# Attention and a top-2 expert layer on one core: the decay moved into the casts of q and k, a router in smaller steps, and late weights cast one part at a time

## The chip, the core and the metric

The kernel runs on one core of a Trainium2 chip. PE is TensorE, which multiplies matrices; DVE is VectorE, ACT is ScalarE, POOL is GpSimd, and SP only issues transfers. Each engine works through its own queue in the order in which the program gives it work, and waits on semaphores for the others. The metric is device time in microseconds (us) for one execution, lower being better; the kernel before was run three times: 549.3, 549.66 and 552.47, median 549.66.

## What is computed

The first half is attention with a decay in place of a softmax, for 8 batches, 8 heads, 576 positions and 64 values a head. The second half sends each of the 4608 tokens to two of eight experts, each two matrix products with a ReLU between.

```python
scores = scale * np.matmul(q, k.transpose(0, 1, 3, 2))
gamma = 1.0 - 2.0 ** (-5.0 - np.arange(H, dtype=np.float32))
Dmat = np.where(rel >= 0, gamma[:, None, None] ** rel[None, :, :], 0.0)
x = np.matmul(scores * Dmat[None], v)          # tokens x 512
noisy = x @ w_gate + np.log1p(np.exp(x @ w_noise)) * noise
# of the two best experts of a token, weights p by softmax:
out[token] += p * (np.maximum(x[token] @ w1[e], 0.0) @ w2[e])
```

The decay gamma^(i-j) for a query at i and a key at j splits into a factor for the query and one for the key.

## The kernel before

The attention is cut into 16 units `u`: a unit is one batch and four heads (two pairs `hp`), of the first 512 positions. The last 64 positions of a batch, its tail, are done for two batches at once (`bp`, four of them). The main loop runs n = 0 to 16; in pass n unit n has its scores and its states computed and unit n - 1 its output. Raw q, k and v are loaded four units ahead on SP's queue, into four buffers each, and `cast(u + 2)` turns them to bf16 two units ahead (`kn`, `vn` in three buffers, `qb` in two):

- k by two selects with a condition that is always true, on POOL (L194), v by a multiply with its share of the decay, gamma^-j, on POOL (L199), q by an ACT copy with the factor 0.125 (L203);
- `tr` (L249, L251) transposes q and k on PE and copies the result from PSUM on ACT (`QT`, `KT`);
- `scores` (L264, L270) multiplies, and DVE applies the causal mask;
- `states` (L286, L292) sums key by value over blocks of positions into `T`, which ACT copies to the block-diagonal `Tb`;
- `out` (L312, L320, L326) brings scores and states together, and DVE multiplies by the query's share of the decay (`gt`) on the way from PSUM to `xT`. `scores_tail` (L337) and `out_tail` (L351) do this for tails, one pair of heads at a time; `cast_tail` (L215 to L221) and `tr_tail` prepare them.

Between these, `step()` stands seven times in a pass. Each call runs the router of a finished batch pair up to its next `yield`. `route` computes logits by PE (L489), the two largest by DVE, the running counts `cum` on POOL (L543), ranks within an expert by a product with a triangular matrix (L576, L578), a payload `pl` for each token (L563 to L568, L628 to L633), a sort key `key` (L612 to L615), one-hot matrices `olo` and `oh` (L642 to L652), and with these, on PE (L658), the list of tokens of each expert. `row` (L483, L484) transposes the tokens back, to go to DRAM as `xd`. A router is put in line at the end of pass 4, 8, 12 and 16.

When three routers are done, the generator `early` is started, which runs five expert tiles of 256 tokens; `more()` gives it one step, at each `step()` of pass 16 and of the loop behind it that ends the last router. Then the token list is finished, indirect DMAs on POOL gather the rows of the first tiles (L823), and `experts` runs the 35 late tiles: `g1` of tile i + 1 is interleaved with `g2` of tile i on PE (L942, L961); the hidden values are evacuated by ACT and DVE in turn (L947, L949) from three `p` buffers; results of first visits go to `yd` by SP, second visits fetch them by an indirect DMA (`prv`, L969), add (L997) and are scattered to the output (L1003).

Weights of experts 2 to 7 come during tiles 0 to 23: `wload(i + 1)` at the end of tile i loads two parts of 512 KB on SP's queue into `wst` (four buffers), and `wcast` at the end of the next tile turns both to bf16 on ACT (L892). Constants are made ahead of the decay tables (`decay_tables`, L110 to L127), among them `gt` of 576 columns for each of eight heads; POOL sets `Tb` to zero (L161) and loads the gate weights with a cast to bf16 (L1105, L1106).

Of the kernel before, what the change touches and what calls it, by code (L numbers as in the profile page):

```python
# [43 lines left out]
HD = 64  # L44
NC9 = 9
# [58 lines left out]
def decay_tables(nc, cp, tmp):  # L104

    vg = cp.tile([P, 2, 2, 4, 2], F32, name="vg")
    vgt = cp.tile([P, 8], F32, name="vgt")
    gt = cp.tile([P, 4, 576], F32, name="gt")
    tv = tmp.tile([P, 576], F32, name="tv", bufs=1)
    nc.gpsimd.iota(tv[:, :512].rearrange("p (c r q) -> p c r q", c=4, r=4), pattern=[[P, 4], [1, 4], [4, 32]],  # L110
                   base=0, channel_multiplier=0, allow_small_or_imprecise_dtypes=True)
    nc.gpsimd.iota(tv[:, 512:], pattern=[[1, HD]], base=512, channel_multiplier=0,
                   allow_small_or_imprecise_dtypes=True)
    sv = tmp.tile([P, 2, 2], F32, name="sv")
    nc.gpsimd.iota(sv, pattern=[[256, 2], [1, 2]], base=0, channel_multiplier=2,
                   allow_small_or_imprecise_dtypes=True)
    st = tmp.tile([P, 1], F32, name="st")
    for b in range(2):
        nc.gpsimd.iota(st[b * HD:(b + 1) * HD], pattern=[[0, 1]], base=512, channel_multiplier=1,
                       allow_small_or_imprecise_dtypes=True)  # L120
    for h in range(8):
        lng = math.log(1.0 - 2.0 ** (-5.0 - h))
        hp, hi = h // 2, h % 2
        s = slice(hi * HD, (hi + 1) * HD)
        nc.scalar.activation(vg[:, h // 4, :, h % 4, :], sv, Act.Exp, scale=-lng)
        nc.scalar.activation(vgt[:, h:h + 1], st, Act.Exp, scale=-lng)
        nc.scalar.activation(gt[s, hp, :], tv[s], Act.Exp, scale=lng)  # L127
    return vg, vgt, gt


class Attention:
# [26 lines left out]
    def tables(self):  # L158
        self.vg, self.vgt, self.gt = decay_tables(self.nc, self.cp, self.bf)
        for t in self.Tb:  # L160
            self.nc.gpsimd.memset(t, 0.0)  # L161
# [24 lines left out]
    def cast(self, u):  # L186

        nc = self.nc
        d = self.u[u]
        hq = self.unit(u)[1]  # L190
        kn = self.bf.tile([P, 2, 2, 4, HD], BF16, name="kn", bufs=3)
        rk = d.pop("rawk").rearrange("p c h (r d) -> p (c h) r d", r=2)
        for r in range(2):
            nc.gpsimd.affine_select(kn[:, r].rearrange("p c h d -> p (c h) d"), rk[:, :, r, :],  # L194
                                    pattern=[[0, 8], [0, HD]], base=1, channel_multiplier=0,
                                    compare_op=Alu.is_gt, fill=0.0)
        vn = self.bf.tile([P, 2, 2, 4, HD], BF16, name="vn", bufs=3)
        rv = d.pop("rawv").rearrange("p c h (r d) -> p (c h) r d", r=2)
        nc.gpsimd.tensor_tensor(vn.rearrange("p r c h d -> p (c h) r d"), rv,  # L199
                                self.vg[:, hq].rearrange("p c h r -> p (c h) r").unsqueeze(3).to_broadcast(  # L200
                                    [P, 8, 2, HD]), Alu.mult)
        qb = self.bf.tile([P, 4, 4, HD], BF16, name="qb")
        nc.scalar.activation(qb.rearrange("p r h d -> p h r d"),  # L203
                             d.pop("rawq").rearrange("p c h w -> p (c h w)").rearrange("p (h r d) -> p h r d", h=4, r=4),
                             Act.Copy, scale=0.125)
        d.update(kn=kn, vn=vn, qb=qb)

    def cast_tail(self, bp):
        nc = self.nc
        d = {}  # L210
        for n in "qk":
            t = self.bf.tile([P, DM], BF16, name=n + "t", bufs=1)
            a = self.tails.pop((n, bp)).rearrange("p h d -> p (h d)")
            if n == "q":
                nc.scalar.activation(t, a, Act.Copy, scale=0.125)  # L215
            else:
# [1007 lines left out]
```

## Time and profile before

| what | value |
|---|---|
| median of three runs | 549.66 us |
| profiled execution | 599.09 us, span 597.5 us |
| granted TensorE clock, mean | 0.847 |
| busy: PE, DVE, ACT, POOL | 454.6, 277.8, 268.2, 274.3 us |
| attention and routers, to the end of unit 15 | 0 to 196.1 us |
| last router, early tiles, first gathers | 196.1 to 270 us |
| late expert tiles | 270 to 580 us |
| moved by DMA | 104.18 MB, 174 GB/s |

The profiled execution is slower than the median, so stages are compared inside it. A busy time is the sum of an engine's instructions in a stretch of time; an engine that is busy for nearly all of a stretch sets its length, while one with much idle time only does so if others wait for it at the wrong moment. In a list of groups the mean duration of one instruction stands behind the busy time, and behind the bar the idle time of the engine ahead of these instructions, with what ended it. The line of an ACT or DVE instruction in a timeline tells which part of which unit is being done.

### The profile page before, as it was taken

Reading aid. Unit: us, or ns where it says so; the run is one execution under the profiler, and the core shown is the slowest. Engines: PE = TensorE matmul, PEld = TensorE weight load, DVE = VectorE, ACT = ScalarE, POOL = GpSimd, SP = SyncE. Lnnn points to the kernel's source line nnn. Section 1 sums busy time; section 2 is a strip of 40 time slices with the busy share of each in tenths; the row PEclk is TensorE's granted clock in tenths of the full one; section 3 lists DMA queues with packets and bytes.
Section 4 is the critical chain, followed back from the end, with each engine's and each line's share of the span. In section 5 each row is a group of like instructions: output and inputs, shape, how many; then the busy total and the mean of one; then the engine's idle time right before and its main releaser. Section 6 shows DMA issues by size and latency. Waiting matters only on the chain.

```text
span 597.5 us, 11717 instructions
## 1 busy us (share of the span) xinstructions
PE 454.6 (76%) x4587; PEld 315.4 (53%) x4627; DVE 277.8 (46%) x770; ACT 268.2 (45%) x381; POOL 274.3 (46%) x350
## 2 busy tenths in 40 slices
PE   0687738828756678968998799799798798989960
PEld 0565626616644455645665366366464464656630
DVE  0266796796778278313333143243233243344430
ACT  5657716723660365534563464464444451312200
POOL 8753543335232605570246216336347256666660
PEclk9989758655875697988999699799799698999995
DMA  9995999709446313730677567577575643544450
GB/s 239 285 238 119 249 297 265 223 0 259 73 72 130 92 41 125 261 118 17 219 257 251 164 218 235 173 253 232 183 269 183 218 135 114 166 129 130 146 176 20
DMA packets 96170, 104.18 MB, mean 174 GB/s; under 512 B 25447, under 2 KB 73065, under 8 KB 96112
## 3 DMA queue, kind: packets, MB, share of 16 engines
q1 hardware_dynamic: 79824, 69.51, 39.4%
q0 software_dynamic: 15232, 32.84, 20.0%
q10 hardware_dynamic: 1056, 1.05, 0.5%
q8 instruction: 37, 0.61, 0.4%
q14 instruction: 21, 0.17, 0.1%
HBM read 84.66 MB, written 28.72 MB: 190 GB/s over the span
## 4 chain that ended last, share of the span: by engine, by line
PE 25%; issue 17%; POOL 5%; DMA 3%; DVE 2%; another core or an unknown queue 1%; POOLq 0%; ACT 0%; DVEq 0%; ACTq 0%
PE p L942 13%; PE po L961 11%; POOL xg L823 3%; DMA xg<-xd,xi 2%; PE pt L926 1%; POOL out_dram L1003 1%; POOL prv L969 1%; DVE o L997 1%; DMA raw_q<-xd,xi 0%; DMA out_dram<-o,ix 0%; DVE hT L949 0%; ACT xgT L929 0%; POOLq L823 0%; ACT hT L947 0%
## 5 line engine op out<-in xcount | busy, mean ns | idle before, releaser
L942 PE MATMUL p<-xgT,w 128*128 128x256 bf16 x1120 | 223.7, 283 | 18.2 <-issue 13.4
L961 PE MATMUL po<-w,hT 128*128 128x512 bf16 x525 | 205.3, 395 | 11.2 <-issue 9.7
L942 PEld LDWEIGHTS <-w 128*128 128x128 bf16 x1120 | 112.8, 101 | 98.8 <-issue 31.8
L949 DVE TENSOR_SCALAR hT<-p 128x512 bf16<-128x512 f32 x70 | 48.3, 691 | 195.3 <-PE p L942 106.0
L947 ACT ACTIVATE hT<-p 128x512 bf16<-128x512 f32 x70 | 41.8, 597 | 173.6 <-remote 62.9
L1003 POOL DMA_INDIRECT out_dram<-o,ix x45 | 45.7, 1016 | 113.3 <-DVE o L997 98.8
L823 POOL DMA_INDIRECT xg<-xd,xi x64 | 66.0, 1032 | 19.2 <-issue 18.6
L961 PEld LDWEIGHTS <-hT 128*128 128x128 bf16 x560 | 56.3, 100 | 26.1 <-issue 17.4
L969 POOL DMA_INDIRECT prv<-yd,ix x45 | 45.6, 1014 | 39.5 <-issue 39.5
L270 DVE TENSOR_TENSOR S<-S,mask 128x512 bf16<-128x512 f32 x64 | 41.1, 683 | 38.5 <-PE S L264 38.5
L892 ACT ACTIVATE w<-wst 128x1024 bf16<-128x1024 f32 x48 | 47.8, 1048 | 0.0
L292 ACT ACTIVATE Tb<-T 64x512 bf16<-64x512 f32 x32 | 18.8, 589 | 44.7 <-PE T L286 44.4
L194 POOL TENSOR_SCALAR_AFFINE_SELECT kn<-raw_k 128x512 bf16<-128x512 f32 x32 | 24.4, 786 | 26.5 <-issue 10.0
L929 ACT ACTIVATE xgT<-pt 128x1024 bf16<-128x1024 bf16 x35 | 35.7, 1020 | 1.6 <-PE pt L926 1.6
L199 POOL TENSOR_TENSOR vn<-raw_v,vg 128x1024 bf16<-128x1024 f32 x16 | 30.9, 1933 | 5.5 <-DMA raw_v<-in_v_dram 1.5
L997 DVE SCALAR_TENSOR_TENSOR o<-po,g,prv 128x512 f32<-128x512 f32 x45 | 31.7, 742 | 3.0 <-DMA prv<-yd,ix 1.7
L336 PE MATMUL S<-TT 64*128 64x128 bf16 x32 | 7.1, 231 | 31.4 <-DVE S L270 20.1
L543 POOL TENSOR_TENSOR cum<-cum,M 128x16 bf16<-128x16 bf16 x36 | 7.8, 217 | 49.8 <-DVE d L548 47.3
L249 PE MATMUL tr<-ident,qb 128*128 128x128 bf16 x128 | 14.1, 277 | 21.4 <-ACT qb L203 16.3
L484 ACT ACTIVATE xr<-tr 128x512 bf16<-128x512 bf16 x36 | 21.2, 598 | 12.6 <-PE tr L483 9.3
L636 POOL COPY xr<-pl 128x24 f32<-128x24 f32 x12 | 12.1, 1048 | 28.1 <-issue 18.8
L251 ACT ACTIVATE QT<-tr 128x1024 bf16<-128x1024 bf16 x16 | 16.4, 1023 | 18.9 <-PE tr L249 18.9
(205 smaller groups left out, 678.6 us busy)
## 6 DMA issues: line engine op xcount, KB each, us to landing
wst<-in_moe_w_dram SPq DMA_DIRECT2D x48, 512.0 KB
raw_k<-in_k_dram SPq DMA_DIRECT2D x32, 256.0 KB
raw_v<-in_v_dram SPq DMA_DIRECT2D x32, 256.0 KB
yd<-y SPq DMA_DIRECT2D x16, 512.0 KB
raw_q<-in_q_dram SPq DMA_DIRECT2D x14, 512.0 KB
xd<-xr SPq DMA_DIRECT2D x12, 396.0 KB
w<-in_moe_w_dram POOLq DMA_DIRECT2D x4, 1024.0 KB
yd<-raw_v SPq DMA_DIRECT2D x5, 512.0 KB
```

The lines of the kernel that those rows point to most:

```text
L199: nc.gpsimd.tensor_tensor(vn.rearrange("p r c h d -> p (c h) r d"), rv, self.vg[:, hq].rearrange("p c h r -> p (c h) r").unsqueeze(3).to_b ...
L270: nc.vector.tensor_tensor(S, p[h], self.K["mask"].unsqueeze(1).to_broadcast([P, 2, 2, P]), Alu.mult)
L823: tc.nc.gpsimd.indirect_dma_start(out=xg[:, s, :], out_offset=None, in_=xd[:, :], in_offset=IOff(ap=keep["xi"][:, j:j + 1], axis=0), bound ...
L892: nc.scalar.activation(W[e][:, k * F:(k + 1) * F], t, Act.Copy)
L929: return lambda: nc.scalar.activation(xgT, pt, Act.Copy)
L942: nc.tensor.matmul(p1[:, f2, :], lhsT=w[:, o:o + P], rhs=xgT[:, di, :], start=(di == 0), stop=(di == KD - 1))
L947: nc.scalar.activation(hT[:, 2 * fp:2 * fp + 2, :], p1, Act.Relu)
L949: V.tensor_relu(hT[:, 2 * fp:2 * fp + 2, :], p1)
L961: nc.tensor.matmul(po[s], lhsT=hT[:, fi, s * P:(s + 1) * P], rhs=w[:, o:o + DM], start=(fi == 0), stop=(fi == KF - 1))
L969: nc.gpsimd.indirect_dma_start(out=prv[i % NP][:, s, :], out_offset=None, in_=yd[:rows, :], in_offset=IOff(ap=st[i]["ix"][:, s, 1:2], axis=0),
L997: V.scalar_tensor_tensor(o[:, s, :], st[i]["po"][s], st[i]["g"][:, s:s + 1], prv[i % NP][:, s, :], Alu.mult, Alu.add)
L1003: ins = nc.gpsimd.indirect_dma_start(out=out[:, :], out_offset=IOff(ap=st[i]["ix"][:, s, 0:1], axis=0), in_=st[i]["o"][:, s, :], in_offset ...
```

## The change

The decay leaves `v` and the output. k is multiplied by gamma^-(j - 288) and q by 0.125 gamma^(i - 288) in their casts, by one POOL multiply each (DVE for units 0 and 1), and v is copied by ACT. The tables are small now (`kg`, `qg`, `tg`), are made ahead of the constants, and DVE sets `Tb` to zero. `xT` is copied from PSUM without a factor, the half e = 1 by DVE and e = 0 by ACT; tails go two pairs of heads at a time, with the output copied by ACT.

The gate weights come in fp32 on ACT's queue and are split by POOL into a bf16 part and the bf16 rest; PE multiplies by both, and DVE adds the two halves of the logits. The router has 25 `yield`s (26 where it also counts ahead) where it had 18 (19): operations are spread over more steps, the nine `row`s among them, one-hot matrices are made for first and second choices in turn, and the payload, the key and some other small operations run on POOL. The rows' write to `xd` follows when the payload is complete, as before.

`wload` takes the next part of a queue; three parts are loaded ahead, and each cast starts the next load. In each of tiles 0 to 23 one part is cast after the evacuation of `xgT` and one after the third evacuation of `hT`.

```diff
+MID = 288
...
-    vg = cp.tile([P, 2, 2, 4, 2], F32, name="vg")
-    vgt = cp.tile([P, 8], F32, name="vgt")
-    gt = cp.tile([P, 4, 576], F32, name="gt")
+    kg = cp.tile([P, 2, 2, 4, 2], F32, name="kg")
+    qg = cp.tile([P, 2, 4, 4], F32, name="qg")
+    tg = cp.tile([P, 2, 8], F32, name="tg")
...
-        nc.scalar.activation(vg[:, h // 4, :, h % 4, :], sv, Act.Exp, scale=-lng)
-        nc.scalar.activation(vgt[:, h:h + 1], st, Act.Exp, scale=-lng)
-        nc.scalar.activation(gt[s, hp, :], tv[s], Act.Exp, scale=lng)
-    return vg, vgt, gt
+        nc.scalar.activation(kg[:, h // 4, :, h % 4, :], sv, Act.Exp, scale=-lng)
+        nc.scalar.activation(qg[:, h // 4, h % 4, :], tv, Act.Exp, scale=lng)
+        nc.scalar.activation(tg[:, 1, h:h + 1], st, Act.Exp, scale=-lng)
+        nc.scalar.activation(tg[:, 0, h:h + 1], st, Act.Exp, scale=lng)
+    nc.vector.tensor_scalar(qg, qg, 0.125, None, Alu.mult)
+    nc.vector.tensor_scalar(tg[:, 0], tg[:, 0], 0.125, None, Alu.mult)
+    return kg, qg, tg
...
-            self.nc.gpsimd.memset(t, 0.0)
+            self.nc.vector.memset(t, 0.0)
...
-        for r in range(2):
-            nc.gpsimd.affine_select(kn[:, r].rearrange("p c h d -> p (c h) d"), rk[:, :, r, :],
-                                    pattern=[[0, 8], [0, HD]], base=1, channel_multiplier=0,
-                                    compare_op=Alu.is_gt, fill=0.0)
+        eng.tensor_tensor(kn.rearrange("p r c h d -> p (c h) r d"),
+                                d.pop("rawk").rearrange("p c h (r d) -> p (c h) r d", r=2),
+                                self.kg[:, hq].rearrange("p c h r -> p (c h) r").unsqueeze(3).to_broadcast(
+                                    [P, 8, 2, HD]), Alu.mult)
         vn = self.bf.tile([P, 2, 2, 4, HD], BF16, name="vn", bufs=3)
-        rv = d.pop("rawv").rearrange("p c h (r d) -> p (c h) r d", r=2)
-        nc.gpsimd.tensor_tensor(vn.rearrange("p r c h d -> p (c h) r d"), rv,
-                                self.vg[:, hq].rearrange("p c h r -> p (c h) r").unsqueeze(3).to_broadcast(
-                                    [P, 8, 2, HD]), Alu.mult)
+        nc.scalar.activation(vn.rearrange("p r c h d -> p (c h) r d"),
+                             d.pop("rawv").rearrange("p c h (r d) -> p (c h) r d", r=2), Act.Copy)
         qb = self.bf.tile([P, 4, 4, HD], BF16, name="qb")
-        nc.scalar.activation(qb.rearrange("p r h d -> p h r d"),
-                             d.pop("rawq").rearrange("p c h w -> p (c h w)").rearrange("p (h r d) -> p h r d", h=4, r=4),
-                             Act.Copy, scale=0.125)
+        eng.tensor_tensor(qb.rearrange("p r h d -> p h r d"),
+                                d.pop("rawq").rearrange("p c h w -> p (c h w)").rearrange(
+                                    "p (h r d) -> p h r d", h=4, r=4),
+                                self.qg[:, hq].unsqueeze(3).to_broadcast([P, 4, 4, HD]), Alu.mult)
...
+        for j, n in enumerate("qk"):
+            t = d[n] = self.bf.tile([P, 8, HD], BF16, name=n + "t", bufs=1)
+            nc.gpsimd.tensor_tensor(t, self.tails.pop((n, bp)),
+                                    self.tg[:, j].unsqueeze(2).to_broadcast([P, 8, HD]), Alu.mult)
+        t = d["v"] = self.bf.tile([P, 8, HD], BF16, name="vt")
+        nc.scalar.activation(t, self.tails.pop(("v", bp)), Act.Copy)
...
-            gv = self.gt[:, 2 * hq:2 * hq + 2, :512].rearrange("p y (c e t) -> p y c e t", c=2, e=2)[:, :, :, e, :]
-            nc.vector.tensor_tensor(xv, p[e], gv, Alu.mult)
+            if e:
+                nc.vector.tensor_copy(xv, p[e])
+            else:
+                nc.scalar.activation(xv, p[e], Act.Copy)
...
+        S = t["S"] = self.sp.tile([P, 2, 2, P], BF16, name="St")
+        p = [self.ps.tile([P, 2, P], F32, name="S", bufs=2) for h in range(2)]
+        for y in range(2):
+            T = t["T"][:, 2 * hq + y]
+            for h in range(2):
+                s = slice(h * HD, (h + 1) * HD)
+                nc.tensor.matmul(p[h][:, y, :], lhsT=T[s, 1, :], rhs=T[s, 0, :], start=True, stop=True)
         for h in range(2):
+            nc.vector.tensor_tensor(S[:, :, h, :], p[h], self.K["maskt"].rearrange("p r q -> p (r q)").unsqueeze(
+                1).to_broadcast([P, 2, P]), Alu.mult)
...
+        nc.scalar.activation(self.xT[bp][:, 2 * hq:2 * hq + 2, 8, :], p.rearrange("p y b t -> p y (b t)"), Act.Copy)
...
-                nc.tensor.matmul(pg[:, c, :], lhsT=xT[:, di, c, :], rhs=self.wgn[:, di, :],
-                                 start=(di == 0), stop=(di == KD - 1))
+                nc.tensor.matmul(pg[:, c].rearrange("p s e -> p (s e)"), lhsT=xT[:, di, c, :],
+                                 rhs=self.wgn[:, di].rearrange("p s e -> p (s e)"), start=(di == 0), stop=(di == KD - 1))
...
+        V.tensor_copy(lg, pg[:, :, 1])
+        V.tensor_add(lg, lg, pg[:, :, 0])
...
+        G = nc.gpsimd
+        G.memset(pl[:, :, 7], 0.0)
+        G.tensor_tensor(pl[:, :, 1], d, df, Alu.add)
+        G.tensor_tensor(r, r, df, Alu.subtract)
+        G.tensor_tensor(pl[:, :, 2], r, pl[:, :, 1], Alu.subtract)
+        G.tensor_scalar(pl[:, :, 0], w[:, 1], -1.0, float(E), Alu.mult, Alu.add)
+        G.tensor_copy(pl[:, :, 3], K["tok"][:, bp])
+        yield
+        row(6)
...
+        G.tensor_scalar(pl[:, :, 5:7], ovt, -1.0, 1.0, Alu.mult, Alu.add)
+        G.tensor_tensor(pl[:, :, 4], py, pl[:, :, 5], Alu.mult)
+        yield
...
+        V.tensor_scalar_min(hib, hi, float(P - 1))
+        yield
...
+        for j in range(2):
+            sh = [P, C, P]
+            V.tensor_tensor(olo[:, j], K["iota"].unsqueeze(1).to_broadcast(sh),
+                            lo[:, j].unsqueeze(2).to_broadcast(sh), Alu.is_equal)
+            yield
+            sh = [P, C, NH]
+            V.tensor_tensor(oh[:, j, :, 0, :], K["iota"][:, :NH].unsqueeze(1).to_broadcast(sh),
+                            hib[:, j].unsqueeze(2).to_broadcast(sh), Alu.is_equal)
+            yield
+            V.tensor_tensor(oh[:, j, :, 1, :], oh[:, j, :, 0, :],
+                            K["cols"][:, c0:c0 + C].unsqueeze(2).to_broadcast(sh), Alu.mult)
+            V.tensor_scalar_mul(oh[:, j, :, 0, :], oh[:, j, :, 0, :], K["pidx"][:, 0:1])
+            yield
+
+        key = self.keep["key"][:, :, c0:c0 + C]
+        G.tensor_scalar(key, w, -KEY, KEY * E + 1.0, Alu.mult, Alu.add)
+        G.tensor_tensor(key, key, rc.rearrange("p c a -> p a c"), Alu.add)
+        G.tensor_tensor(key, key, ov, Alu.mult)
+        G.tensor_scalar(key, key, -1.0, None, Alu.add)
...
+        queue = [(e, k) for e, j in (loads[i] for i in sorted(loads)) for k in (2 * j, 2 * j + 1)]
+        AHEAD = 3
+
+        def wload():
+            if not queue:
+                return
+            e, k = queue.pop(0)
+            t = stg.tile([P, F], F32, name="wst")
...
+            parts.append((e, k, t))
...
+            e, k, t = parts.pop(0)
-            for k, t in parts.pop(i):
-                nc.scalar.activation(W[e][:, k * F:(k + 1) * F], t, Act.Copy)
+            nc.scalar.activation(W[e][:, k * F:(k + 1) * F], t, Act.Copy)
+            wload()
...
-            wload(0)
+            for _ in range(AHEAD):
+                wload()
...
-                    cb = lambda: comb(i - 1)
-                    a = g1(i + 1, {0: ev, 1: cb}) if i + 1 < NT else iter(())
+                    def first():
+                        ev()
+                        wcast(i)
+                    a = g1(i + 1, {0: first, 1: lambda: comb(i - 1), 2: lambda: wcast(i)}) if i + 1 < NT else iter(())
...
-                wcast(i)
-                wload(i + 1)
...
+        at.tables()
         K = at.K = constants(nc, cp)
-        at.tables()
-        wgn = cp.tile([P, KD, 2 * E], BF16, name="wgn")
-        nc.gpsimd.dma_start(out=wgn[:, :, :E], in_=moe_w_gate.rearrange("(do di) e -> di do e", di=P))
-        nc.gpsimd.dma_start(out=wgn[:, :, E:], in_=moe_w_noise.rearrange("(do di) e -> di do e", di=P))
+        wg32 = at.bf.tile([P, KD, 2 * E], F32, name="wg32", bufs=1)
+        nc.scalar.dma_start(out=wg32[:, :, :E], in_=moe_w_gate.rearrange("(do di) e -> di do e", di=P))
+        nc.scalar.dma_start(out=wg32[:, :, E:], in_=moe_w_noise.rearrange("(do di) e -> di do e", di=P))
+        wgn = cp.tile([P, KD, 2, 2 * E], BF16, name="wgn")
...
-        at.cast(0)
+        at.cast(0, nc.vector)
+        nc.gpsimd.tensor_copy(wgn[:, :, 0], wg32)
+        nc.gpsimd.tensor_tensor(wgn[:, :, 1], wg32, wgn[:, :, 0], Alu.subtract)
...
+        at.cast(1, nc.vector)
```

The `yield`s that are added elsewhere in `route` stand behind a `row`, a maximum, a product or a sum, one each, with no other work.

## The prediction

> **What bounds the kernel now.** I first put the profiled execution beside the median: 599.09 us around a span of 597.5, against a median of 549.66. All durations below are from that one execution, so the sum is made against 599.09 and then scaled by 549.66/599.09 = 0.9175; the profile doesn't show which stage loses the 49 us. Then I cut the span into stages with the table of windows. In the timeline the evacuation of the attention states (`Tb`, L292, one pair for each unit) marks the end of each of the 16 units, so I asked for windows from one mark to the next, n = 5 to 12.
>
> ```profile
> core 0: us, PE busy (x) PEld busy (x) DVE busy (x) ACT busy (x) POOL busy (x), PEclk, DMA share, GB/s
> 54.35:67.02 12.67, 8.87 (x188) 7.33 (x186) 7.96 (x26) 9.93 (x16) 5.29 (x13) 0.85 0.73 188
> 67.02:86.87 19.85, 8.36 (x139) 6.32 (x137) 18.83 (x54) 6.26 (x11) 10.32 (x11) 0.59 1.00 252
> 86.87:96.17 9.30, 8.59 (x146) 7.20 (x147) 7.65 (x12) 4.80 (x6) 5.49 (x3) 0.62 1.13 327
> 96.17:102.83 6.66, 5.26 (x132) 4.01 (x131) 4.66 (x10) 5.09 (x7) 3.17 (x3) 1.00 1.00 238
> ...
> 102.83:115.01 12.18, 9.61 (x183) 7.58 (x182) 7.87 (x26) 9.92 (x15) 1.55 (x8) 0.69 0.89 250
> 115.01:136.06 21.05, 9.85 (x141) 7.69 (x140) 20.03 (x54) 6.34 (x11) 10.85 (x13) 0.50 0.18 53
> 136.06:148.38 12.32, 10.01 (x147) 8.20 (x148) 8.47 (x17) 4.80 (x6) 6.23 (x4) 0.50 1.09 257
> 148.38:155.93 7.55, 6.75 (x132) 5.35 (x131) 4.75 (x10) 5.08 (x6) 4.05 (x4) 0.77 0.34 47
> ```
>
> Read it as a period of four units. A router call (`route`) is threaded through the steps of the three units after a batch pair ends. In the second of them VectorE is busy 18.83 of 19.85 us and 20.03 of 21.05; PE, ACT and DMA have slack in the second period (0.18 of DMA there). The first of the three is nearest to ACT (9.93 of 12.67). The unit without a router takes 6.7 to 7.6. So one period costs 48.5 us (n = 5..8), then 53.1 (n = 9..12), then 40.2 for n = 13..15, which ends at 196.10.
>
> The timelines of VectorE and of GpSimd inside the long unit show small router operations of 0.17 us that last 1.85, next to a GpSimd multiply of 1.90:
>
> ```profile
> 116.75 1.85 DVE L558 TENSOR_TENSOR df<-df,low 128x9 f32<-128x9 f32 x1
> 119.81 1.88 DVE L568 COPY pl<-tok 128x9 f32<-128x9 f32 x1
> 130.91 2.55 DVE L642 TENSOR_TENSOR olo<-iota,lo 128x2304 bf16<-128x2304 bf16 x1
> 134.42 2.48 DVE L647 TENSOR_TENSOR oh<-iota,hib 128x1440 bf16<-128x1440 bf16 x1
> ```
> ```profile
> 116.68 1.90 POOL L199 TENSOR_TENSOR vn<-raw_v,vg 128x1024 bf16<-128x1024 f32 x1
> 119.77 1.90 POOL L199 TENSOR_TENSOR vn<-raw_v,vg 128x1024 bf16<-128x1024 f32 x1
> ```
>
> After 196 the last router and five early expert tiles run until 270, and from 270 to 580 the 35 late tiles: there PE is busy 275.12 of 310 us. In the groups of instructions the casts of the late weights stand with no idle time before them, and PE's largest waits in the matmul group name "issue", not ACT:
>
> ```profile
> L942 PE MATMUL p<-xgT,w 128*128 128x256 bf16 x1120 | 223.7, 283 | 18.2 <-issue 13.4 <-DVE hT L949 1.9 <-DVE isB L910 0.4
> L892 ACT ACTIVATE w<-wst 128x1024 bf16<-128x1024 f32 x48 | 47.8, 1048 | 0.0
> ```
>
> **The change, part by part.** *VectorE's work for a unit.* Two `xT` multiplies (L326, 682 ns each by the groups, 0.64 back to back) become one copy on VectorE and one on ACT. No PSUM-to-SBUF copy of this shape is shown on VectorE; I take the multiply's 0.64, bounded by it above and by ACT's 0.60 for 512 elements. VectorE thus does 3.2 us a unit where it did 3.9 (four masks at 0.64 stay), ACT 0.6 more. In the two units of a period with tails, eight masks of 128 (286 ns) become four of 256, which I put at 0.4 each, between 0.29 (L337) and 0.68 (L270), and four 288 ns multiplies become two ACT copies of 256, some 0.37 each.
>
> *The router in small steps.* Counting `yield`s: 18 (19 with the counts) become 25 (26), and seven steps run per unit, so a router ends in the fourth unit and not in the third. Some 13 small VectorE operations a router go to POOL (the five `pl` ones and their memset, four `key`, `py`, two late `pl`), about 2.2 us; the maximum of `hi` and its cast become one, and a second addition to `lg` is new (0.29, as L494). VectorE's router work is then, at one operation each 0.27 or 0.2 as the timeline spaces them: first unit (logits, two maxima) 3.9, second (masks, thresholds, weights, ranks) 4.8, third (indices, 2.6 + 1.65 + 1.68 + 0.6 of one-hots less the last part) 7.8, fourth 2.4.
>
> *Casts.* For each unit POOL did two selects (0.63 each) and a multiply of 1.9, 3.2 us; now it does two multiplies, 3.8. ACT changes a cast of q (1.05) for one of v with the same number of elements. The q transposes now wait for the second of the two POOL operations, and in the router's second unit these are behind `pl` operations that wait for VectorE's `df`. They are needed half a unit later or more, in the next unit, and 1.1 + 3.8 us fits in that; without that cover the PE would stand up to 4 us there. ACT's new cast of v waits for the last of the three loads. POOL's waits for raw_v sum to only 1.5 us, but with KT and Tb queued behind ACT the price where it happens is up to 4 us; I count it in the range.
>
> *A rule against it.* The row above (1.85 us for nine elements beside a 1.90 POOL multiply) is a VectorE operation held for the whole of a GpSimd one. The Trainium skill, "SBUF — State Buffer", section "SBUF: two separate sides", says so: the shared pair is an exclusive lock, taken for the whole instruction, against VectorE operations with two SBUF inputs or in a two-port mode. By the rows, the excess of L553, L557, L558, L564, L566, L568, L589 and L647 over their undisturbed durations is about 12 us for all routers, a third of the 35 us that POOL spends casting in the 11 router units. At a third of 42 us it becomes 14: 2 us more. By the rule alone every multiply could hit a waiting operation, 42 us, which is 30 more than now and would eat the gain. I take the rows, and 1.5 us per router unit in the second and third: POOL's new in-order wait for `df` also keeps it idle while the `df` chain runs.
>
> *Units after.* First: ACT loses one exponential with its table load (1.28 + 0.21) and one row evacuation (0.6), gains 0.6, 9.93 to 8.4; with the 2.4 us that it now lies above ACT, 10.8. Second: VectorE 3.2 + 0.8 + 4.8 + 1.5 = 10.3, ACT 9.8 (three casts and evacuations 3.1, Tb 1.2, xT 0.6, exponential 1.5, four rows 2.4, tails 1.0); above both by one more us or two, 12. Third: 3.2 + 7.8 + 1.5 and 0.5, 13. Fourth: 6.4 and one, 7.5. A period is 43.3 where it was 48.5 and 53.1, and 35.8 for the last three units where it was 40.2: -5.2 - 9.8 - 4.4 = -19.4 us. Loads allow it: at some 250 GB/s, a unit's 1.57 MB are 6.3 us.
>
> *The start.* Small tables replace eight exponentials of 0.67 us (-5 on ACT), but the four memsets of Tb (0.9 each) stand on VectorE ahead of the constants' memsets and of the two first casts, and POOL's selects of constants wait for them; the first qb comes about when it did (15.9). The tail casts of q and k, both on POOL in n = 0, hold tr_tail 1.6 us longer. I take +1.5, bounds -3 and +4. The gate weights, now in two halves from fp32, cost two POOL operations and matmuls 32 wide for 16 (170 ns each now): below 1 us.
>
> *After unit 15.* Router 2 now ends 5 us after unit 15 (it had ended with it), the early tiles begin that much later, but one tile's work no longer stands between it and router 3: its first call comes 11 us after unit 15, not 14.5 (210.6 - 196.1). Router 3 then has 25 steps, each followed by a step of the early tiles on PE, 38 us where 18 steps took 33. Together +2. Behind it stand the 16 gathers on POOL at 1.31 us, in both kernels; the smaller rest of PE work there doesn't show.
>
> *The late weights.* The same 48 casts of 1.05 us, now after xgT and after the third `hT` of a tile. ACT is busy 129.76 of 310 and PE has three `p` buffers, so a block of 2.1 us at the tile's end held PE little: PE's waits for "ACT" don't appear in the L942 row. Loads come singly, three parts ahead in four buffers; SP gains no wait, since a buffer is free when it asks. SP's queue of y writes stays short. Zero, bounds -4 and +4 for gathers that meet these bursts (two stalls of 6.1 us on an xg gather lie in the chain of waits, at 320 and 413).
>
> Sum: -19.4 + 1.5 + 2 = -15.9, so 583.2 for the profiled execution and 535 for the median.
>
> **Rivals.** *ACT becomes the bound (slower).* If in the router units ACT and not VectorE decides, moving half of `xT` and the tails' copies there costs 0.6 + 0.3 us in each of 15 units, +13.5, and the seven extra steps another +2; no relief for VectorE counts. That gives 599.09 + 15.5, times 0.9175, 564. It decides from the point where ACT's queue, with its wait for raw_v, is longer than VectorE's in the second unit: for it speaks 9.93 of 12.67 in the first unit, against it 6.3 of 20 in the second.
>
> *The lock takes the gain back.* 10 to 15 us more blocked VectorE time: 545 to 549, no change. *Loads bound sooner.* The first period has DMA at 0.95, raw_v waits at 73 us; if that floor holds, its 5.2 us go, and 540 remains. *More gain.* The two later periods fall to VectorE's sums alone (3.2 + 3.9, 9, 11, 6.4, some 34 us each): 9 us more for each, and 520 is left. *The edit at the late weights does matter*, if gathers are the reason for PE's stalls: 4 us either way, inside the range.
>
> **Numbers.** About what a measurement can tell from no change is 1%, 5.5 us. The forecast with its variants of load bound and more gain: 0.62. Lock takes it back: 0.14. ACT bound, slower: 0.24. The range of the likely case alone is 520 to 544; over all it must reach into the slower case, 520 to 560.
>
> **What would show it.** VectorE below 13 us busy in every router unit, and no unit above 14 us; unit 15's Tb near 178 in place of 196; router 3's first logits some 11 us after it; the late tiles still 310 us. Wrong if ACT shows 11 us busy in the first router unit with the `KT` evacuation behind a cast of v that waits for its load, if PE's q transposes wait for POOL's `qb`, or if the router's fourth unit delays the early tiles by more than it saves.

## The result, and the profile after

The changed kernel takes 529.78 us (median of four, 528.2 to 531.05), beside 550.92 us for the kernel before (four runs in turn with it, 549.3 to 552.47): a ratio of 0.9615, 95% interval 0.9566 to 0.9664, so 21 us less. The forecast was 535, in a range of 520 to 560.

First the windows of the changed kernel, cut as those of before: from the `Tb` evacuation (now L285) of one unit to that of the next, n = 5 to 12, then the rest. Columns as before: time, then busy us and count of each engine, granted clock, DMA share, GB/s.

```profile
core 0: us, PE busy (x) PEld busy (x) DVE busy (x) ACT busy (x) POOL busy (x), PEclk, DMA share, GB/s
53.19:65.03 11.84, 8.54 (x166) 7.09 (x166) 8.22 (x14) 8.89 (x15) 3.80 (x3) 0.66 0.93 276
65.03:75.02 9.99, 6.87 (x140) 5.10 (x128) 9.37 (x32) 8.10 (x13) 4.37 (x16) 0.82 0.95 267
75.02:82.64 7.62, 7.62 (x132) 5.79 (x133) 7.38 (x18) 6.08 (x9) 6.67 (x11) 0.56 1.12 340
82.64:100.91 18.27, 10.64 (x150) 8.42 (x149) 15.42 (x19) 5.79 (x7) 12.19 (x8) 0.57 1.03 297
100.91:113.55 12.64, 9.56 (x192) 7.83 (x194) 6.54 (x20) 8.91 (x14) 3.76 (x2) 0.64 0.69 212
113.55:122.29 8.74, 7.70 (x140) 6.25 (x132) 7.54 (x25) 8.09 (x12) 3.70 (x16) 0.68 0.18 52
122.29:129.27 6.98, 5.61 (x132) 4.11 (x131) 6.81 (x16) 6.10 (x9) 6.03 (x10) 1.00 0.01 2
129.27:150.24 20.97, 10.47 (x151) 8.46 (x150) 17.66 (x26) 5.79 (x8) 14.56 (x12) 0.59 0.74 149
150.24:162.61 12.37, 10.00 (x192) 7.94 (x194) 6.64 (x20) 8.89 (x14) 4.50 (x3) 0.64 0.64 104
162.61:170.72 8.11, 7.50 (x140) 5.97 (x132) 6.91 (x24) 7.25 (x11) 3.00 (x15) 0.73 0.01 2
170.72:175.02 4.30, 4.14 (x130) 3.05 (x129) 4.02 (x18) 2.65 (x5) 2.10 (x8) 1.00 0.47 48
...
246.00:510.00 264.00, 257.56 (x1912) 176.92 (x1912) 108.81 (x297) 131.13 (x173) 146.70 (x145) 0.98 0.69 224
```

The second unit of a router (65.03, 113.55) fell from about 20 us to 9 or 10, the third (75.02, 122.29) to 7 or 8. The work went on into the fourth, which was the short one and is now the long one: 18.27 and 20.97 us, with VectorE busy 15.42 and 17.66 of them. The last three units before the mark of unit 15 are light ones, since the heavy fourth unit of that router lies behind it. Unit 15 ends at 175.02.

In the groups of the changed kernel the matmul row has lost its "issue" waits (13.4 us in the row of before), and the casts of the late weights still stand without idle time before them:

```profile
L949 PE MATMUL p<-xgT,w 128*128 128x256 bf16 x1120 | 212.5, 274 | 1.2 <-DVE hT L956 1.2
...
L898 ACT ACTIVATE w<-wst 128x1024 bf16<-128x1024 f32 x48 | 50.6, 1053 | 0.0
```

It looks as if those 13 us of PE's waits were removed by the edit at the late weights, and as if the late tiles had gained 46 us (264 for 310). Both are wrong, as the first two experiments show.

### The profile page after: what moved, and what is told of

Same layout as the page of the kernel before. It is cut to its first block, busy times and chain, and to the rows that moved or that the text cites. A ratio compares the mean times of both kernels' runs of the same rounds, so it can differ in the third digit from the quotient of the medians.

```text
span 527.1 us, 11727 instructions
## 1 busy us (share of the span) xinstructions
PE 429.3 (81%) x4627; PEld 308.5 (59%) x4627; DVE 272.9 (52%) x696; ACT 276.6 (52%) x413; POOL 286.4 (54%) x377
## 3 DMA queue, kind: packets, MB, share of 16 engines
q10 hardware_dynamic: 2112, 1.08, 0.7%
## 4 chain that ended last, share of the span: by engine, by line
PE 61%; DVE 17%; DMA 7%; ACT 3%; SPq 3%; issue 3%; POOL 3%; POOLq 0%; DVEq 0%; ACTq 0%
PE p L949 23%; PE po L968 22%; DVE S L263 3%; PE pt L933 3%; SPq L174 2%; PE S L392 2%; DMA raw_v<-in_v_dram 2%; PE x L402 2%; DMA raw_q<-xd,xi 2%; DVE olo L643 1%; PE T L279 1%; DVE oh L650 1%; DVE oh L647 1%; PE x L305 1%; DVE oh L652 1%
## 5 line engine op out<-in xcount | busy, mean ns | idle before, releaser
L949 PE MATMUL p<-xgT,w 128*128 128x256 bf16 x1120 | 212.5, 274 | 1.2 <-DVE hT L956 1.2
L968 PE MATMUL po<-w,hT 128*128 128x512 bf16 x560 | 211.3, 382 | 0.0
L949 PEld LDWEIGHTS <-w 128*128 128x128 bf16 x1120 | 110.0, 98 | 73.0 <-issue 3.1
L898 ACT ACTIVATE w<-wst 128x1024 bf16<-128x1024 f32 x48 | 50.6, 1053 | 0.0
L192 POOL TENSOR_TENSOR kn<-raw_k,kg 128x1024 bf16<-128x1024 f32 x14 | 27.1, 1938 | 30.6 <-DMA raw_k<-in_k_dram 15.4
L200 POOL TENSOR_TENSOR qb<-raw_q,qg 128x1024 bf16<-128x1024 f32 x14 | 30.3, 2163 | 0.0
L257 PE MATMUL S<-QT,KT 64*64 64x128 bf16 x512 | 19.1, 271 | 13.1 <-DVE S L263 7.7
L482 PE MATMUL tr<-ident,xT 128*128 128x128 bf16 x144 | 17.3, 256 | 9.8 <-ACT QT L244 8.1
L279 PE MATMUL T<-vn,kn 64*64 64x64 bf16 (+2 forms) x512 | 24.7, 240 | 0.0
L244 ACT ACTIVATE KT<-tr 128x1024 bf16<-128x1024 bf16 x16 | 16.3, 1018 | 13.0 <-PE tr L242 12.9
```

Source lines behind the costliest of these rows:

```text
L200: eng.tensor_tensor(qb.rearrange("p r h d -> p h r d"), d.pop("rawq").rearrange("p c h w -> p (c h w)").rearrange("p (h r d) -> p h r d", ...
L898: nc.scalar.activation(W[e][:, k * F:(k + 1) * F], t, Act.Copy)
L949: nc.tensor.matmul(p1[:, f2, :], lhsT=w[:, o:o + P], rhs=xgT[:, di, :], start=(di == 0), stop=(di == KD - 1))
L968: nc.tensor.matmul(po[s], lhsT=hT[:, fi, s * P:(s + 1) * P], rhs=w[:, o:o + DM], start=(fi == 0), stop=(fi == KF - 1))
```

## The experiments

Each ran beside the kernel before on the same chip; the ratio is to that. Units are named by n, "the mark" of a unit is its `Tb` evacuation.

**The kernel before, once more.** No edit.

> The kernel before, profiled once more. First-half theory: the late tiles took 310 us in the first profile of it because that one execution was disturbed there; another profile shows about 262 us from 270 on, a total near 550, and PE with hardly any idle time in these tiles. Late-weights theory: the two parts cast at a tile's end hold PE up, so that the late tiles take near 310 us again and the total is near 600.

549.08 us in the profiled execution. Its windows, the attention's eleven units n = 5 to 15 as one, the stretch between, and the late tiles,

```profile
core 0: us, PE busy (x) PEld busy (x) DVE busy (x) ACT busy (x) POOL busy (x), PEclk, DMA share, GB/s
55.29:197.22 141.93, 91.34 (x1616) 72.86 (x1616) 112.93 (x301) 68.81 (x98) 56.80 (x75) 0.66 0.72 170
197.22:269.70 72.48, 55.54 (x480) 38.94 (x481) 35.00 (x122) 34.99 (x55) 36.58 (x45) 0.85 0.39 127
269.70:531.00 261.30, 256.50 (x1904) 176.15 (x1902) 108.93 (x294) 130.26 (x173) 144.63 (x143) 0.99 0.67 220
```

and its matmul row of the late tiles:

```profile
L942 PE MATMUL p<-xgT,w 128*128 128x256 bf16 x1120 | 212.7, 274 | 1.2 <-DVE hT L949 1.2
```

The late tiles take 261.3 us with PE busy 256.50, and the "issue" waits are gone, as in the changed kernel. So the 310 us of the profile shown ahead of the prediction are not the kernel's own. They belong to that execution or to the chip that it ran on, which isn't on record: its 599.09 us, and 325.7 us from the first `po` matmul (271.75) to the end, are like those of the third chip met below. The marks of units 4 to 15 agree within 1.2 us from one execution to the other. From here on this second trace stands for "before". Measured from the first `po` matmul of a late tile (`po` is the second of an expert's two products) to the end of the span, before takes 278.1 us and after 277.4.

**The change with the old handling of late weights.**

```diff
-                    a = g1(i + 1, {0: first, 1: lambda: comb(i - 1), 2: lambda: wcast(i)}) if i + 1 < NT else iter(())
+                    cb = lambda: comb(i - 1)
+                    a = g1(i + 1, {0: ev, 1: cb}) if i + 1 < NT else iter(())
...
+                wcast(i)
+                wload(i + 1)
```

> The changed kernel with the late weights loaded and cast as before (two parts at a tile's end). First-half theory: no difference to the changed kernel beyond 0.5%, 527 to 532 us, ratio to before 0.96. Late-weights theory: most of the gain goes, 545 us or more.

529.38 us (6 runs), ratio 0.9623 [0.9582, 0.9664], against 0.9615 with the edit. Late part 278.1 us. The edit at the late weights is worth nothing that these runs can tell.

**The two other parts, one at a time.** The first kernel is before with the decay in the casts, the small tables, the plain `xT` copies and the wide tails, but the old router, gate weights and late weights. The second is before with the new router and the split gate weights alone.

```diff
-        nc.gpsimd.tensor_tensor(vn.rearrange("p r c h d -> p (c h) r d"), rv,
...
+        eng.tensor_tensor(kn.rearrange("p r c h d -> p (c h) r d"),
...
+        eng.tensor_tensor(qb.rearrange("p r h d -> p h r d"),
```
```diff
+        G = nc.gpsimd
...
+        G.tensor_tensor(pl[:, :, 1], d, df, Alu.add)
...
+        yield
```

> Only the decay in the casts, the small tables and the tails: the router, the gate weights and the late weights as before. If the relief of VectorE in every unit carries the gain (0.64 us in 15 units, 10 us, and the tails): 538 to 542. If the spreading of the router carries it: 547 to 551, or slower for POOL's longer casts.

> Only the router in small steps with its POOL operations and the gate weights in two halves: attention, tables and late weights as before. If the spreading carries the gain: 533 to 540. If the relief by the decay carries it: 545 to 551. If the two add up, this one and the decay alone together save 21 us.

The decay alone: 554.79 us, 1.0108 [1.0057, 1.016], slower by about 1%. The router alone: 530.02 us, 0.9661 [0.9609, 0.9713], which overlaps with the whole change. So the router carries the gain. The decay takes one operation of about 0.64 us a unit off VectorE, 7 us over units 5 to 15, yet unit 15 ends at 203.61 where it ended at 197.22. Of these 6.4 us 2.9 were there at the mark of unit 4 (58.19 for 55.29); units 5 to 15 took 145.4 us for 141.9. The timeline of VectorE in the decay-alone kernel, early in a router's second unit:

```profile
70.36 0.22 DVE L551 RECIPROCAL r<-r 128x9 f32<-128x9 f32 x1
70.61 1.73 DVE L552 TENSOR_TENSOR d<-d,r 128x9 f32<-128x9 f32 x1
...
72.37 1.83 DVE L556 TENSOR_TENSOR df<-r,d 128x9 f32<-128x9 f32 x1
74.24 1.83 DVE L557 TENSOR_TENSOR df<-df,low 128x9 f32<-128x9 f32 x1
...
76.10 1.83 DVE L563 TENSOR_TENSOR pl<-d,df 128x9 f32<-128x9 f32 x1
```

and that of GpSimd in the same stretch:

```profile
70.42 1.90 POOL L192 TENSOR_TENSOR kn<-raw_k,kg 128x1024 bf16<-128x1024 f32 x1
72.27 1.91 POOL L200 TENSOR_TENSOR qb<-raw_q,qg 128x1024 bf16<-128x1024 f32 x1
74.15 1.90 POOL L192 TENSOR_TENSOR kn<-raw_k,kg 128x1024 bf16<-128x1024 f32 x1
76.00 1.90 POOL L200 TENSOR_TENSOR qb<-raw_q,qg 128x1024 bf16<-128x1024 f32 x1
```

Four operations on nine elements, 0.17 us when undisturbed, each end with one of GpSimd's multiplies. The casts of two units came in a row, and for their 7.5 us the router's chain moved on by little more than one operation for each.

**The router's two halves.** The router-alone kernel with the payload and key operations back on VectorE, and the same with seven of the added `yield`s removed (18 or 19 steps again).

```diff
# payload and key on VectorE
-        G = nc.gpsimd
+        G = nc.vector
# coarse steps
         row(0)
-        yield
         lg = sp.tile([P, C, 2 * E], F32, name="lg")
...
```

> The kernel with only the new router (530 us), but its thirteen small operations of payload, key and row index back on VectorE: spread without relief by POOL. Spread theory: what counts is that one-hots and ranks no longer stand in one unit and that router 2's heavy part falls behind unit 15; 530 to 535. Relief theory (2.2 us of VectorE a router, and POOL's copies of the payload that no longer wait for VectorE): 537 or more.

> The same new router with POOL's operations, but seven yields taken out, so that it has 18 (19) steps again and ends in the third unit of a period. Spread theory: 543 to 551, close to before. Relief theory: 530 to 535, close to the new router whole.

Without GpSimd's share 537.96 us, 0.9772 [0.9725, 0.9819], unit 15 at 189.82. With coarse steps 534.39 us, 0.9711 [0.9653, 0.9769], unit 15 at 186.89. On this chip before took 549.39. So the steps alone bring about 11.4 us, the relief by GpSimd about 15.0, each with the other rearrangements of the router, and both together 20.1 (550.15 - 530.02 on the other chip). Both kernels came out where the relief theory had put them (537 or more, 530 to 535), and the coarse one far from the 543 to 551 of the spread theory. Yet without the relief more than half of the gain stays. The two overlap, and neither is the cause by itself; what the rearrangements bring without either wasn't tried.

**GpSimd casts q first.** The decay-alone kernel with `qb` made ahead of `kn`, so that the q transposes wait for one multiply and not two.

```diff
+        qb = self.bf.tile([P, 4, 4, HD], BF16, name="qb")
+        eng.tensor_tensor(qb.rearrange("p r h d -> p h r d"),
...
         eng.tensor_tensor(kn.rearrange("p r c h d -> p (c h) r d"),
...
-        qb = self.bf.tile([P, 4, 4, HD], BF16, name="qb")
-        eng.tensor_tensor(qb.rearrange("p r h d -> p h r d"),
```

> The decay alone (554.8 us), with POOL casting q ahead of k. If the decay alone is slower because PE's q transposes wait for qb as the second POOL cast behind the payload copies that wait for VectorE (the third unit of a period took 15.0 us where it took 9.3): 2 us in three to six units come back, 546 to 551. If the loss is POOL's longer hold of the port against VectorE: no change, 553 to 556.

553.53 us, 1.008 [1.0046, 1.0114]; decay alone was 1.0108 [1.0057, 1.016]. No difference that can be told, and the third unit of the first router still takes 14.8 us (15.0). The order of the two casts isn't what costs.

**The casts of the decay on VectorE.** The decay-alone kernel with every k and q multiply on VectorE and none on GpSimd.

```diff
-        eng = eng or nc.gpsimd
+        eng = nc.vector
```

> The decay alone (554.8 us) with all casts of k and q on VectorE (1.27 us each, with no other instruction) and none on POOL. If VectorE's own work is the price: 2.5 us in each of the eleven units with a router, 575 to 583. If POOL's casts against the port hold VectorE up about as long as doing them would take: 550 to 558.

594.17 us (two runs), on a third chip where before takes 601.21: ratio 0.9887 [0.9847, 0.9928], against 1.0108 for GpSimd's casts on the other chip. The forecasts in us were made for the other chips and can't be read against it. Unit 15 ends at 193.40 instead of 203.61. The same chain of operations in VectorE's timeline of this kernel:

```profile
70.80 0.17 DVE L552 TENSOR_TENSOR d<-d,r 128x9 f32<-128x9 f32 x1
...
71.01 0.17 DVE L556 TENSOR_TENSOR df<-r,d 128x9 f32<-128x9 f32 x1
71.21 0.17 DVE L557 TENSOR_TENSOR df<-df,low 128x9 f32<-128x9 f32 x1
...
71.42 0.17 DVE L563 TENSOR_TENSOR pl<-d,df 128x9 f32<-128x9 f32 x1
```

Each takes 0.17 us. The windows of n = 5 to 15, first of the decay alone, then of this kernel:

```profile
58.19:203.61 145.42, 91.19 (x1616) 71.92 (x1616) 111.36 (x270) 76.06 (x116) 62.04 (x64) 0.64 0.68 163
```
```profile
58.06:193.40 135.34, 92.64 (x1632) 73.53 (x1629) 112.35 (x288) 76.56 (x115) 34.77 (x46) 0.68 0.73 175
```

VectorE was given 18 casts more (two in each of passes 5 to 13), 22.0 us in all, and its busy time rose by 1.0 us only. What it gave up is held time. I added that up: for every VectorE operation of these units, what it took above the shortest of the same form in any of seven traces, where that is over 0.1 us. This gives about 14 us for before, 21.8 for the decay alone, 2.1 with the casts on VectorE, 12.3 for the router alone and 18.8 for the whole change. So the decay alone adds nearly 8 us of held time, which is about what it takes off VectorE (7 us): busy time fell from 112.93 to 111.36 only.

The 10.1 us between the two windows above are VectorE's idle time (the window less its busy time), 34.1 us in the first and 23.0 in the second. Its waits for scores from PE went from 22.5 to 13.7 us, those for ACT's exponential `d` from 7.3 to 1.0. Two causes fit this. The exclusive lock of the prediction lengthens the chain on which the others wait; and with the casts on VectorE the q and k transposes no longer wait for GpSimd, of which only the order of the two casts, above, was tried. So in units 5 to 15 GpSimd's multiplies are the price of the decay, by traces of two chips; in which of the two ways it is paid isn't shown. The later start is not theirs: the mark of unit 4 comes at 58.06 without them and at 58.19 with them.

**Both halves of `xT` on VectorE.** The changed kernel with this edit.

```diff
-            if e:
-                nc.vector.tensor_copy(xv, p[e])
-            else:
-                nc.scalar.activation(xv, p[e], Act.Copy)
+            nc.vector.tensor_copy(xv, p[e])
```

> The changed kernel with both xT copies on VectorE (0.68 us more in each unit there, 0.6 less on ACT). If the relief of VectorE by ACT is worth its size where VectorE is the bound: 533 to 538. If ACT's queue has become as long: 527 to 531.

587.42 us, 0.9769 [0.9722, 0.9817]; unit 15 at 181.53, with 22.2 us held. This is the chip of the kernel just above, where before takes 601.21 us (599.12 to 606.28), and the changed kernel itself didn't run there. From the mark of unit 4 to that of unit 15 this kernel takes 127.8 us (53.77 to 181.53), the changed kernel elsewhere 121.8. The router-alone code, which ran on both chips, takes 125.4 on the one and 127.0 on the other. So ACT's half of `xT` seems to be worth some 4 to 6 us in these units, by single traces from two chips, and nothing speaks for ACT as the bound.

**Two prefetched tiles instead of three.** In the changed kernel PE stands still just ahead of the late tiles. Its timeline:

```profile
239.83 3.44 PE L949 MATMUL p<-xgT,w 128*128 128x256 bf16 x30
248.47 0.59 PE L933 MATMUL pt<-ident,raw_q 128*128 128x128 bf16 x4 [5.20 <-DMA raw_q<-xd,xi]
249.28 0.61 PE L933 MATMUL pt<-ident,raw_q 128*128 128x128 bf16 x4 [0.22 <-DMA raw_q<-xd,xi]
249.68 0.63 PE L968 MATMUL po<-w,hT 128*128 128x512 bf16 x1
251.51 0.58 PE L949 MATMUL p<-xgT,w 128*128 128x256 bf16 x2 [1.20 <-DVE hT L956]
```

The three tiles gathered ahead of the others go into `raw_q` buffers, which the early tiles use too. In GpSimd's timeline the third one's two gathers are issued at 241.42 and 242.73, behind six gathers into `xg` buffers for later tiles. With two such tiles the third goes into an `xg` buffer.

```diff
-        for i in range(3):
+        for i in range(2):
```

> The changed kernel with the third late tile gathered into its own buffer of the late tiles and not into one that an early tile holds until its end. If the 5.2 us that PE waits for that gather before the late tiles is the price of this order: 523 to 526, faster than the changed kernel by 3 to 6 us. If POOL's sixteen gathers at 1.31 us bound the start whatever their order: no change, 528 to 531.

519.61 us (516.61 to 520.35, 6 runs), 0.9452 [0.9414, 0.949], faster than both kernels and by more than was written ahead. PE's timeline of this kernel at the same place:

```profile
240.03 3.66 PE L949 MATMUL p<-xgT,w 128*128 128x256 bf16 x32
243.53 0.61 PE L933 MATMUL pt<-ident,xg 128*128 128x128 bf16 x8
243.97 0.38 PE L968 MATMUL po<-w,hT 128*128 128x512 bf16 x1
244.19 0.38 PE L949 MATMUL p<-xgT,w 128*128 128x256 bf16 x2
```

The wait is gone and the first `po` comes 5.7 us earlier. Behind it, from that `po` to the end of the span, 273.7 us are left instead of 277.4: the wait had also slowed what followed. In the changed kernel's windows of the wait itself, of what follows and of the time after that,

```profile
243.30:248.40 5.10, 0.00 (x0) 0.00 (x0) 0.00 (x0) 0.00 (x0) 3.88 (x5) 0.71 0.97 342
248.40:255.70 7.30, 5.81 (x24) 3.07 (x25) 2.50 (x11) 1.00 (x2) 0.57 (x1) 0.50 0.31 122
255.70:263.00 7.30, 7.30 (x57) 5.13 (x56) 2.84 (x9) 3.93 (x6) 0.00 (x0) 1.00 0.22 74
```

the granted clock is 0.50 in the 7.3 us after the wait, and 1.00 later. In the two-tile kernel, without the wait, it is 1.00 in the 7.3 us from its first `po`:

```profile
243.97:251.27 7.30, 7.30 (x58) 5.06 (x56) 1.29 (x3) 4.34 (x6) 3.96 (x4) 1.00 1.02 377
```

From the first `po` on, eleven steps of PE take 2.39 us here (243.97 to 246.36) and 6.05 in the changed kernel (249.68 to 255.73). These are the 3.7 us behind the first `po`: 1.2 are a second wait, for `hT`, and the rest is the halved clock. The kernel before waits at this place too, 4.19 us, so this isn't part of the change's effect.

**Two tiles on the router alone, and one-hots scaled by ACT.** The router-alone kernel with the edit above, and the two-tile kernel with the product by `pidx` moved from VectorE to ACT. Both ran on the chip where before takes 601.21.

```diff
-            V.tensor_scalar_mul(oh[:, j, :, 0, :], oh[:, j, :, 0, :], K["pidx"][:, 0:1])
+            nc.scalar.activation(oh[:, j, :, 0, :], oh[:, j, :, 0, :], Act.Copy, scale=K["pidx"][:, 0:1])
```

> The new router and the gather into an own buffer, with attention, tables, tails and late weights as before. If the decay in the casts adds nothing once the router is spread: 518 to 522, as the changed kernel with that gather (519.6). If it adds the half per cent by which the two ratios differ: 522 to 526.

> The changed kernel with the gather into an own buffer, and the scaling of the one-hots by the row number (0.43 to 1.95 us, twice a router) moved from VectorE to ACT, which is busy 5.8 of 18 us in the unit that holds the one-hots. If VectorE still sets that unit: 2 us a router come back in three routers, 512 to 517. If the unit is set by POOL's casts against VectorE's port, or the later one-hot only waits for ACT: 518 to 522.

Router with two tiles: 592.44 us, 0.9882 [0.9825, 0.9939], so 8.8 us saved where the router alone, with three tiles, saved 20.1 elsewhere. One-hots on ACT: 578.48 us, 0.964 [0.9603, 0.9676]. Neither ratio can be set beside those of the other chips. The late tiles of this second kernel:

```profile
248.26:560.00 311.74, 276.84 (x1879) 179.99 (x1911) 106.97 (x287) 130.46 (x173) 144.75 (x143) 0.93 0.58 184
```

They take 311.74 us, as the 310 of the first profile of before. From the first `po` to the end all four kernels of this chip take 325.1 to 327.7 us, where those of the other two take 273.7 to 278.1. The stretch ahead, from the last router's first logits to the first `po`, is longer too: 60.6 and 65.7 us in these two kernels, for 51.2 in the two-tile kernel and 53.3 in the router alone elsewhere. The last router's first logits come at 188.51 with the one-hots on ACT, 192.76 in the two-tile kernel: about 4 us, across chips, and no more than the 4.2 us that one code differs by (which was the slower one here). That edit is promising and not shown. The two kernels of this chip differ by the decay in the casts, the late weights and that product, and the first `po` comes at 249.14 against 265.40. On the chip where both ran, router alone and whole change (with old late weights) were level, 530.02 and 529.38. Whether the decay adds to the new router stays open.

## Why the prediction was right, and where it wasn't

The direction, the size and the place (the units and their routers) came out. Several terms did not, and they offset each other, so the size is in part luck. Against the second trace of before, by single traces:

| step | forecast, us | measured, us | how |
|---|---|---|---|
| start, to the mark of unit 4 | +1.5 | -2.1 | 53.19 - 55.29 |
| units 5 to 8 | -5.2 | -0.9 | 47.72 - 48.65 |
| units 9 to 12 | -9.8 | -3.8 | 49.33 - 53.10 |
| units 13 to 15 | -4.4 | -15.4 | 24.78 - 40.18 |
| after unit 15 to the first `po` | +2 | +2.4 | 74.66 - 72.23 |
| late tiles | 0 | -0.7 | 277.4 - 278.1 |
| sum | -15.9 | -20.4 | spans 527.1 - 547.5 |

- **The start** was mis-sized, and with 3.6 us it is most of the 4.5 us that the sum lacks; a us or so of it is spread, since the kernels with old weights and with two tiles, which start alike, pass the mark at 54.55 and 52.74. I set the tables' 5 us gain against the `Tb` memsets and let the first `qb` come as before. The memsets took 485 ns each on VectorE, not 0.9 us, and the first `QT` evacuation comes at 13.91 us for 17.03. GpSimd's constants did wait for VectorE as foretold (6.97 us at 9.22), which cost nothing.
- **The units** sum to -20.1 against -19.4, but by a wrong distribution. The step that failed is the one that took VectorE's work of a pass for the window that ends at that pass's mark: "third 13, fourth 7.5". The steps were counted rightly, and all one-hots but the last two products stand in pass 7, the router's third unit. But ACT's mark of unit 7 (82.64) does not wait for VectorE, which was behind it in its queue:

```profile
83.44 1.34 DVE L643 TENSOR_TENSOR olo<-iota,lo 128x1152 bf16<-128x1152 bf16 x1
84.71 1.27 DVE L263 TENSOR_TENSOR S<-S,mask 128x512 bf16<-128x512 f32 x2
...
89.89 0.90 DVE L647 TENSOR_TENSOR oh<-iota,hib 128x720 bf16<-128x720 bf16 x1
90.72 1.27 DVE L263 TENSOR_TENSOR S<-S,mask 128x512 bf16<-128x512 f32 x2
```

  The masks at 84.71 are unit 7's own second ones, those at 90.72 unit 8's first, so some 8 us of VectorE's work of pass 7 fall into the fourth window, which takes 18.27 (20.97 in the next period). The kernel with one-hots scaled by ACT confirms it: there ACT's queue waits for them ahead of the mark, and with the first one-hot at 82.31 the same two windows take 13.88 and 10.57. The two together were also too small, 20.5 us forecast for 25.9 and 28.0. By the count above VectorE was held in them for 6.2 and 6.5 us, where I had 1.5. So "VectorE below 13 us busy in every router unit, and no unit above 14 us" was wrong. In units 13 to 15 the one-hots fall behind the mark of unit 15 (VectorE works on them from 175.19 to 183.44), where before had them ahead. That is why this stretch gained 15.4 and not 4.4, and why the next step was dearer at first.
- **The decay's relief** (VectorE 3.2 us a unit for 3.9) stood in the sum of every unit and isn't found in the time. Alone, the decay made the kernel 1% slower; beside the new router nothing of it can be told (530.02 and 529.38). The gain that the sum shared out over both came with the router.
- **The lock.** I weighed the row of before against the rule in the Trainium skill, "SBUF — State Buffer", section "SBUF: two separate sides": the row gave 14 us of held VectorE time for the whole change, the rule alone 42. It was 18.8, nearer to the row but above it. VectorE's timeline shows two small operations and one of the one-hots:

```profile
81.76 1.77 DVE L636 TENSOR_SCALAR hib<-hi 128x18 bf16<-128x18 f32 x1
...
93.35 1.95 DVE L652 TENSOR_SCALAR oh<-oh,pidx 128x720 bf16<-128x720 bf16 x1
...
121.82 1.75 DVE L602 TENSOR_TENSOR prs<-prf 128x72 f32<-128x72 f32 x1
```

  and GpSimd's shows the other direction, which I hadn't counted, beside one-hots of 0.9 to 1.4 us:

```profile
81.59 1.90 POOL L192 TENSOR_TENSOR kn<-raw_k,kg 128x1024 bf16<-128x1024 f32 x1
83.46 3.09 POOL L200 TENSOR_TENSOR qb<-raw_q,qg 128x1024 bf16<-128x1024 f32 x1
```

  A multiply that takes 1.90 undisturbed took 3.09. Both fences fit the page's rule that the first to start keeps the shared pair for its whole instruction.
- **After unit 15** the total was right by two errors. The last router's first logits come 17.5 us after the mark (192.49 - 175.02), not 11, since the displaced one-hots run first; its 25 steps then took 32.4 us (192.49 to 224.91), about the 31.8 of before, and not the 38 that I gave them.
- **The late weights** at zero: right, by the kernel with the old handling. **The scaling** by 0.9175 was wrong in kind: the 49 us were lost nearly all in the late tiles of that execution, which the change hardly touches, so nothing of a difference ahead of them should be scaled, and "the late tiles still 310 us" failed as a sign. Unscaled, the same sum gives 549.66 - 15.9 = 533.8.
- **Rivals.** ACT as the bound: its wait for a load did come, at its longest ahead of unit 4's mark,

```profile
51.32 1.06 ACT L197 ACTIVATE vn<-raw_v 128x1024 bf16<-128x1024 f32 x1 [4.47 <-DMA raw_v<-in_v_dram]
```

  but from n = 5 to 14 ACT is busy 5.8 to 8.9 us of units of 7 to 21, and the start was still faster. The lock that takes all back comes near to what the decay alone shows (+1.08%, 21.8 us held), as far as the lock is the reason there; the router outweighed it. That VectorE's own sums alone decide (520) didn't come about either.

## What to carry to other kernels

Before a stage is summed, profile twice: an execution that is 9% off the median can have lost it in one stage that the change doesn't touch, and a whole chip can be like that. A chain of small operations that is threaded through steady work gains both from finer steps and from giving some of them to an idle engine, and the two gains overlap. A mark on one engine doesn't end another's work: look in the timeline at where each engine stands in its queue before a window is taken for a unit. A cast that goes to GpSimd because VectorE is the bound must be priced by what it holds on VectorE and by who waits for it: here moving 18 casts back cost VectorE 22.0 us of its own work and only 1.0 us of busy time, and these units became 10.1 us shorter, between two chips.

## What the runs showed of the hardware

- A wait of 5.2 us on PE cost about 9.4 us in all (5.7 before the first `po`, 3.7 behind it, with a second wait of 1.2 in them): the granted clock was 0.50 for the next 7.3 us (1.00 there without the wait), in which the `po` matmuls and pairs of `p` matmuls follow each other by 0.43 us instead of 0.22.
- GpSimd and VectorE hold each other both ways: nine elements in 1.83 us for 0.17 on VectorE, a multiply in 3.09 for 1.90 on GpSimd.
- The same kernel took 549 to 551 us on two chips and 601 on a third, and there the late tiles of all four kernels that were profiled take some 50 us more, at a granted clock of 0.93 (one-hots by ACT) for 0.98 (the changed kernel elsewhere). What makes that chip's late tiles slower wasn't found.
